# Full-array matmuls that may run as two half-width products side by side, so that the array keeps its column tiling

## The chip, the cores and the metric

The kernel runs on one NeuronCore of a Trainium2 chip. The metric is device time in microseconds for one launch, the median of several executions. The engines are named as in the profile: PE is the matrix engine (TensorE), PEld its weight loads, DVE the vector engine, ACT the scalar engine, POOL the GpSimd engine, SP the engine that issues most DMAs.

## What is computed

The input `x` has 2048 tokens of 576 features. It goes twice through a pair of blocks, with the same weights both times. Block A is attention over segments of 32 tokens with 8 memory tokens that are carried from segment to segment; block B is a gated MLP. Cut to what matters:

```
def A(x):                                  # x: 2048 x 576, already normalised
    mem = mem0                             # 8 x 576
    for s in range(64):                    # segments of 32 tokens
        h = concat(mem, x[32*s : 32*s+32])             # 40 x 576
        q, k, v = h @ Wq, h @ Wk, h @ Wv               # 32 heads of 128
        p = softmax(mask(q @ k.T * 128**-0.5))         # 40 x 40 per head
        o = (p @ v) @ Wo                               # 40 x 576
        mem, out[s] = o[:8], o[8:]
def B(x): return (silu(x @ w1) * (x @ w3)) @ w2        # 576 -> 4608 -> 576
x = x + A(layernorm(x)); x = x + B(layernorm(x))       # first layer
x = x + A(layernorm(x)); x = x + B(layernorm(x))       # second layer, same weights
```

A segment needs the memory rows of the segment before it, so the 64 steps of one layer are a chain.

## The kernel before

**Tiling and stages.** Time is cut into 72 steps `t`. In step `t` the kernel works on segment `t` of the first layer and on segment `t - 8` of the second (`LAG = 8`), as far as both exist; the two sit side by side, so that most products have 80 moving columns (2 x 40). In the first and the last steps only one layer is there and the products have 40. Per step there are four groups of eight heads, and for each group: Q and K projections (`QK`, 64 products with 128 contracted rows in two nodes, and `QKt`, the remaining 64 rows, as pairs in row tiling), scores (`SC`), softmax on DVE and ACT, a transposition of the probabilities as a matmul (`TR`), the product with V (`PV`), and the output projection (`WO`, 32 products, and `WOt`, the last 64 of the 576 output features, eight half-width products in column tiling). V itself is projected by `VX`, `VM` (column tiling) or `VG` (full array, with a row-tiled rest). Every four steps a piece of the MLP of both layers (`FF`, `FFt`, then `W2`, `W2b`) is spread between the attention work. Layer norms and the residual are transposed on PE too (`tr`, `POST`).

**Tiling of the array.** A matmul here uses the whole array (128 columns of weights), or a half of its columns (64 wide, at output partition 0 or 64: column tiling), or a half of its rows (64 contracted rows: row tiling), or quarters and smaller. Each PE node has a `mode` that says which: "full", "col", "row", "c32", "oct", "quad".

**What sets the order.** `make_nodes` makes a graph of nodes, each with an engine, a duration that is assumed, and what it needs and frees. `plan` walks through it. The order on PE is written out by hand: `ORDER` is a string with one letter for each PE node (`KINDS` gives the letters: Q, q, S, T, P, O, o, F, f, W, w, G, g, ...), made of `FIRST` (805 letters), eleven times `FOUR` (224 letters, four steps each) and `LAST` (684). For the other engines `plan` takes whichever node can start first by its assumed times; nodes of the kind "AD" (copies out of PSUM) go to ACT or DVE, whichever is free first. `plan` adds `SWITCH` (0.098 us) where the mode of a PE node differs from that of the one before. The emitter `Emitter` then writes the instructions in that order, each engine in program order; `mm` writes one matmul, and all PE instructions carry the line of that helper (L578; L581 is ACT's helper, L584 DVE's, L587 SP's, L593 POOL's).

**The end.** The last MLP piece has no attention beside it. Its weights don't go through the small double buffers, but are loaded into the space of Wq/Wk/Wv (`W`, `WV`) by `tail_load` in eight pieces of 512 columns, as soon as the last step has used that space. The finished rows are cast to bf16 by ACT (`fin_cast`) and stored.

Of the kernel before, what the change touches and what calls it, by code (L numbers as in the profile page):

```python
# [51 lines left out]
class Node:  # L52
# [3 lines left out]
    def __init__(self, eng, dur, fn, deps=(), prio=0.0, mode=None, acq=(), rel=(), name="", lat=None):  # L56
        self.eng, self.dur, self.fn, self.prio, self.mode = eng, dur, fn, prio, mode
        self.deps = [d for d in deps if d is not None]
        self.acq, self.rel, self.name = list(acq), list(rel), name
        self.lat = lat if lat is not None else (PE_LAT if eng == "PE" else EW_LAT)  # L60
        self.outs, self.ready, self.start, self.end, self.by = [], 0.0, None, None, None
        self.left = len(self.deps)
# [13 lines left out]
def plan(nodes, pools, letters):  # L76
# [16 lines left out]
    mode = None  # L93
    order = []
    at = 0
# [18 lines left out]
    while len(order) < len(nodes):  # L114
        best = None
        for e in t_eng:
            if e == "PE":
                cands = seq[at:at + 1] if at < len(seq) and seq[at].left == 0 else []
            else:
                cands = ready[e] + (both if e in ("ACT", "DVE") else [])  # L120
            if not cands:
                continue
            ests = [(est(e, n), n) for n in cands]
            t = min(x for x, _ in ests)
            if t >= NOW:
                continue
            if best is None or t < best[0]:
                best = (t, e, ests)
        if best is None:
            raise RuntimeError(f"the plan is stuck at {at}: {seq[at].name}")  # L130
        t, e, ests = best
        st, n = min((x for x in ests if x[0] <= t + 1e-9), key=lambda x: x[1].prio)
        dur = n.dur
        if isinstance(dur, tuple):
            dur = dur[0] if e == "ACT" else dur[1]
        if e == "PE":
            at += 1
            if n.mode != mode:
                dur += SWITCH
                mode = n.mode  # L140
        elif n.eng == "AD":
            both.remove(n)
        else:
            ready[e].remove(n)
        n.start, n.end, n.by = st, st + dur, e
        t_eng[e] = n.end
        for s in n.acq:
            if s.i is not None:
                continue
            f = free[s.pool]  # L150
            s.i = min((i for i in range(len(f)) if f[i] <= st + 1e-9), key=lambda i: f[i])
            f[s.i] = NOW
        for s in n.rel:
            s.users -= 1
            s.end = max(s.end, n.end + (PE_LAT if e == "PE" else EW_LAT))
            if s.users == 0:
                free[s.pool][s.i] = s.end
        for m in n.outs:
            m.ready = max(m.ready, n.end + (0.0 if m.eng == e == "PE" else n.lat))
            m.left -= 1  # L160
            if m.left == 0:
                push(m)
        order.append(n)
    return order
# [58 lines left out]
def make_nodes(em, nseg, pools, o=Opt, dma_bw=230e3, load_bw=400e3):  # L223
# [32 lines left out]
    m0t = node("PE", 0.3, em.m0_tr(b[0]), deps=[ld_m0], prio=-5, mode="full", acq=b, name="m0tr")  # L256
# [9 lines left out]
    def ln_nodes(tag, src, xn, deps, prio, writes, warm=False):  # L266

        a = node("DVE", 1.16, em.ln_stats(src, xn), deps=deps, prio=prio, acq=[] if src is xn else [xn], name=tag + "stats")
        p_ = node("POOL", 0.45, em.ln_pow(xn), deps=[a], prio=prio, name=tag + "pow")
        c = node("DVE", 0.46 if src is xn else 0.66, em.ln_norm(src, xn), deps=[p_], prio=prio, name=tag + "norm")  # L270
        b = Slot("bank", users=len(writes))
        d = node("PE", 5 * 0.056, em.ln_tr(xn, b, warm), deps=[c], prio=prio, mode="full", acq=[b], rel=[xn], name=tag + "tr")
        out = []
        for wr, cost, more in writes:
            out.append(node("AD", cost, wr(b), deps=[d] + more + out[-1:], prio=prio, rel=[b], name=tag + "wr"))
        return out
# [22 lines left out]
    def v_nodes(name, t, k, prio, tail_at, emit, strips, deps, tail_deps, free):  # L299
# [6 lines left out]
        for r in (0, 1):  # L306
            outs = em.v_parts(strips, r)
            b[r].users = len(outs)
            for p0, width, row, blk in outs:
                e = node("AD", ew(512), em.v_ev(b[r], p0, width, row, blk), deps=[m_, n] + free.get(blk // 2, []), prio=prio + 0.01 * (blk // 2),  # L310
                         rel=[b[r]], name=name + "e")
                vx_ev.setdefault((name, t, blk // 2), []).append(e)
# [6 lines left out]
    def vg_nodes(t, g, deps, tail_deps):  # L319
# [4 lines left out]
        m_ = node("PE", 8 * 0.2158, em.vg(t, g, b, False), deps=deps, prio=t + o.vm, mode="full", acq=b, name="VG")  # L324
# [5 lines left out]
    def vg_out(t, g, b, deps, row):  # L330

        return [node("AD", ew(512), em.v_ev(b[r], row, R64, row, 2 * g + r), deps=deps, prio=t + o.vm + 0.01 * g + (0.05 if row == 0 else 0.0), rel=[b[r]],
# [11 lines left out]
    def step(t):  # L344
# [17 lines left out]
        for g in range(NG):  # L362
            qs, qe = [], []
            for u in (2 * g, 2 * g + 1):
# [4 lines left out]
                          prio=pq, mode="full", acq=[q] + b, name="QK")  # L369
# [11 lines left out]
            sc = node("PE", 8 * 0.0165 * nl, em.scores(t, g, qs, s), deps=qe, prio=pf + o.sc, mode="col", acq=[s, sme], rel=qs, name="SC")  # L381
# [9 lines left out]
            tr = node("PE", 8 * mm80, em.ptr(t, g, pb, bt), deps=[pbs], prio=pf + o.tr, mode="full", acq=[pts] + bt, name="TR")  # L391
            node("POOL", 1.2, em.pb_zero(pb), deps=[tr], prio=pf, rel=[pb], name="pbz")
            pe_ = [node("AD", ew(4 * c80), em.pt_ev(t, g, m, bt[m], pts), deps=[tr], prio=pf, rel=[bt[m]], name="PTe") for m in (0, 1)]
            if paired(t):
# [6 lines left out]
                      prio=pf + o.pv, mode="full", acq=b + [ot], rel=[pts], name="PV")  # L401
# [4 lines left out]
            wo = node("PE", 32 * mm80, em.wo(t, g, ot), deps=ote + ([ld_o[g]] if t == 0 else []), prio=t + o.wo + o.wog * g, mode="full",  # L406
# [9 lines left out]
        if t == nst - 1:  # L416
            last_reads[2].extend(wos)
# [14 lines left out]
    def post(li, g):  # L432
# [4 lines left out]
                 prio=prio, mode="full", acq=b, name="POST")  # L437
# [3 lines left out]
    last_reads = [], [], []  # L441
    kept = {}

    def job(j):
# [18 lines left out]
        if last:  # L463
            v_done, qk_done, wo_done = last_reads
            tail = []
            for i in range(8):
                late = wo_done[i - 4:i - 3] if i >= 4 else []
                parts = [(0, 9 * 512, qk_done[2 * i:2 * i + 2] + late), (1, 4 * 576, v_done + late)]
                tail.append([load("tail", kb(128, c), s0 + o.tail_at + 0.01 * i, em.tail_load(i, what), deps=dep) for what, c, dep in parts])

        npp = NPR // 2
        for at, pp in enumerate([npp - 1] + list(range(npp - 1)) if last else range(npp)):
            mids, w2s, htts, lds = [], [], [], []
            stays = last and pp == npp - 1
            for pr_ in (2 * pp, 2 * pp + 1):
# [18 lines left out]
                fm = node("PE", 16 * mm, em.ffn_up(ents, pr_, w13, b, last and not stays, False), deps=wr + ld, prio=prio, mode="full",  # L494
# [8 lines left out]
            for (bi, g) in ents:  # L503
                b = banks()
                d = node("PE", 8 * 0.1225, em.ffn_down(bi, pp, htts, w2s, b, last and not stays), deps=mids + lds, prio=prio + o.w2,
                         mode="full", acq=b, rel=htts + w2s, name="W2b" if bi else "W2")
                es = [node("DVE", dve(288), em.ffn_add(g, h, xr[g], b[h]), deps=[d], prio=prio + o.w2, rel=[b[h]], name="W2a")
                      for h in (0, 1)]
                w2_last[bi] = es
        for (bi, g) in ents:  # L510
            if bi == 0:
                ht_set(1, g, ln_nodes("L1", xr[g], Slot("xn"), w2_last[0], s0 + LAG - 4.2, ht_writes(1, g)))
            else:
                xn = Slot("xn")
                c = node("ACT", actc(576), em.fin_cast(xr[g], xn), deps=w2_last[1], prio=s0 + LAG - 4.2, acq=[xn], rel=[xr[g]], name="fin")
                node("SWD", 1.0, em.store(g, xn, last), deps=[c], prio=s0 + LAG - 4.2, rel=[xn], lat=3.0, name="store")
# [42 lines left out]
class Emitter:  # L559


    def __init__(self, nc, tc, T, aps, nseg):
# [4 lines left out]
        self.tail_w, self.ys = {}, {}  # L567
# [9 lines left out]
    def mm(self, out, lhsT, rhs, start, stop, **k):  # L577
        self.ch("PE", self.nc.tensor.matmul(out, lhsT=lhsT, rhs=rhs, start=start, stop=stop, skip_group_check=True, **k))  # L578
# [107 lines left out]
    def tail_load(self, i, what):  # L686

        def f(n):
            T = self.T
            fa = i * 512  # L690
            t13, t2 = T.W[:, :, fa:fa + 512], T.WV[:, i * 4 * D:(i + 1) * 4 * D].rearrange("p (b d) -> p b d", b=4)
            if what != 1:
                for kind, wd in ((0, self.a.w1), (1, self.a.w3)):
                    self.dma(t13[:, 4 * kind:4 * kind + 4], wd[0:4 * P, fa:fa + 512].rearrange("(c p) f -> p c f", p=P))
                for kind, wd in ((0, self.a.w1), (1, self.a.w3)):
                    self.dma(t13[kind * R64:(kind + 1) * R64, 8], wd[4 * P:D, fa:fa + 512])
            if what != 0:
                self.dma(t2, self.a.w2[fa:fa + 512, :].rearrange("(b p) d -> p b d", p=P))
            for h in range(2):
                self.tail_w[2 * i + h] = (t13[:, :, h * 2 * P:(h + 1) * 2 * P], t2[:, 2 * h:2 * h + 2])  # L700
# [213 lines left out]
    def scores(self, t, g, qs, s):  # L914

        def f(n):
            S = self.bk(s)[:, 0:GH * QW].rearrange("p (h k) -> p h k", h=GH)
            both = self.both(t)
            for hl in range(4):
                for ab in (0, 1):  # L920
                    Q = self.T.QKT[:, qs[ab].i].rearrange("p a h n -> p (a h n)")
                    for kd in ((0, 1) if both else (0,)):
# [3 lines left out]
                                True, True, tile_position=(0, 64 * kd))  # L926
# [231 lines left out]
    def ffn_add(self, g, half, xr, b):  # L1158
        def f(n):
            X = self.T.XR[:, xr.i, half * 288:(half + 1) * 288]  # L1160
            self.v("scalar_tensor_tensor", X, self.bk(b)[:, 0:288], 0.5, X, op0=ALU.mult, op1=ALU.add)
        return f

    def fin_cast(self, xr, xn):
        return lambda n: self.act(self.T.XN[:, xn.i, 0:D], self.T.XR[:, xr.i, :], ACT.Copy)
# [10 lines left out]
def kernel(  # L1176
# [88 lines left out]
    for n in plan(nodes, pools, ORDER):  # L1265
        n.fn(n)
# [35 lines left out]
```

## Time and profile before

| | |
|---|---|
| median of 3 runs | 2701.22 us (2698.18 to 2702.51) |
| the profiled execution | 2705.47 us, of which its span is 2703.5 us |
| PE | 97% busy, 55,714 matmuls and 55,795 weight loads |
| DVE / ACT / POOL | 77% / 51% / 12% busy |
| granted PE clock | 0.992 |
| DMA | 321.40 MB, mean 119 GB/s |

The profile is one execution. A busy PE in it is a modelled figure: the end of a matmul is computed, so matmuls that follow each other closely overlap in the listing (one of 80 columns is listed with some 200 ns), and the distance from start to start tells the pace. The timeline view merges neighbours of the same kind, with the number of instructions after an x.

### The profile page before, as it was taken

How to read it: one execution, taken by the hardware profiler on the slowest of the kernel's cores; microseconds unless marked ns; L12 is line 12 of the kernel's file. 1: busy time of each engine (PE TensorE's matmuls, PEld its weight loads, DVE VectorE, ACT ScalarE, POOL GpSimd, SP SyncE). 2: the span in 40 equal slices, each digit the busy share in tenths (PEclk: the TensorE clock that was granted, in tenths of full speed). 3: DMA queues.
4: the chain of work that ended last, by engine and by line, in shares of the span. 5: the costliest groups of instructions: out<-in, count | busy, mean ns of one | idle time of the engine just before them, and what ended most of it. 6: DMA issues, size and time to landing. Idle time of an engine off the chain costs nothing.

```text
span 2703.5 us, 126553 instructions
## 1 busy us (share of the span) xinstructions
PE 2629.8 (97%) x55714; PEld 2227.4 (82%) x55795; DVE 2089.3 (77%) x5376; ACT 1370.6 (51%) x4025; POOL 333.5 (12%) x400
## 2 busy tenths in 40 slices
PE   5999999999999999999999999999999999999998
PEld 3788888888888888888888888888888888888886
DVE  4778887887778778777877877787787777787876
ACT  2655554544546454454645445464544546454553
POOL 1111110110101011010101101010110101011110
PEclk7999999999999999999999999999999999999999
DMA  9064534334343333434333343433334342434358
GB/s 316 4 176 120 158 89 119 88 110 125 93 131 88 115 92 110 125 95 130 87 114 93 110 125 93 131 88 112 94 110 125 93 131 71 125 97 135 117 164 258
DMA packets 483224, 321.40 MB, mean 119 GB/s; under 512 B 26376, under 2 KB 477328, under 8 KB 482160
## 3 DMA queue, kind: packets, MB, share of 16 engines
q1 hardware_dynamic: 479488, 306.22, 38.7%
q8 instruction: 436, 7.14, 1.1%
q0 software_dynamic: 3024, 6.93, 0.9%
q14 instruction: 116, 0.95, 0.1%
q10 hardware_dynamic: 160, 0.16, 0.0%
HBM read 308.49 MB, written 2.36 MB: 115 GB/s over the span
## 4 chain that ended last, share of the span: by engine, by line
PE 87%; ACT 4%; DMA 4%; DVE 3%; issue 1%; SPq 0%; POOL 0%; DVEq 0%; ACTq 0%; POOLq 0%
PE bank L578 87%; ACT V L581 3%; DMA W<-in_B_w_dram 2%; DVE SME L584 1%; DMA W<-in_A_Wk_dram 1%; DMA WV<-in_A_Wv_dram 1%; DVE STAT L584 1%; DVE V L584 1%; ACT SME L581 0%; SPq L587 0%; DMA W2C<-in_B_w_dram 0%; ACT XTB L581 0%; ACT PTS L581 0%; ACT QKT L581 0%; DVE PB L584 0%
## 5 line engine op out<-in xcount | busy, mean ns | idle before, releaser
L578 PEld LDWEIGHTS <-W 128*128 128x128 bf16 (+1 forms) x29520 | 1238.8, 98 | 150.6 <-issue 44.2
L578 PE MATMUL bank<-HT,W 128*128 128x80 bf16 (+3 forms) x23040 | 812.4, 197 | 23.7 <-DMA W<-in_A_Wq_dram 10.5
L578 PE MATMUL bank<-XTB,W 128*128 128x256 bf16 (+3 forms) x6480 | 661.3, 261 | 8.1 <-DMA W<-in_B_w_dram 6.9
L581 ACT ACTIVATE QKT<-bank 128x256 bf16<-128x256 f32 (+3 forms) x1587 | 367.6, 318 | 372.7 <-PE bank L578 353.8
L981 POOL MEMSET PB<- 128x1024 bf16 x288 | 274.1, 952 | 1820.1 <-PE bank L578 1317.4
L578 PE MATMUL bank<-OT,WO 128*128 128x80 bf16 (+3 forms) x11520 | 407.1, 198 | 1.1 <-issue 0.5
L581 ACT ACTIVATE V<-bank 64x512 bf16<-64x512 f32 (+1 forms) x616 | 347.3, 586 | 109.4 <-PE bank L578 104.2
L578 PEld LDWEIGHTS <-WO 128*128 128x128 bf16 (+1 forms) x11520 | 379.8, 102 | 16.1 <-issue 6.0
L578 PE MATMUL bank<-WV,HT 128*32 128x512 bf16 (+5 forms) x3160 | 356.9, 385 | 13.9 <-issue 8.5
L578 PE MATMUL bank<-W2C,HTT 128*128 128x288 bf16 x2240 | 315.4, 286 | 0.3 <-DMA W2C<-in_B_w_dram 0.2
L584 DVE TENSOR_TENSOR PB<-SME,STAT 40x128 bf16<-40x128 f32 (+4 forms) x912 | 274.8, 335 | 14.9
L584 DVE TENSOR_REDUCE STAT<-SME 104x8 f32<-104x320 f32 (+1 forms) x576 | 274.0, 476 | 13.9 <-ACT SME L581 8.5
L581 ACT ACTIVATE HTT<-bank 128x512 bf16<-128x512 f32 (+1 forms) x324 | 180.0, 557 | 180.7 <-PE bank L578 178.7
L578 PEld LDWEIGHTS <-HT 128*32 128x32 bf16 (+4 forms) x3240 | 137.1, 96 | 157.0 <-issue 38.5
L584 DVE SCALAR_TENSOR_TENSOR XR<-bank,XR 128x288 f32<-128x288 f32 x576 | 246.5, 450 | 15.8 <-PE bank L578 7.9
L578 PEld LDWEIGHTS <-HTT 128*128 128x128 bf16 x2304 | 209.8, 98 | 49.1 <-issue 0.9
L581 ACT ACTIVATE OT<-bank 128x320 bf16<-128x320 f32 (+1 forms) x398 | 149.7, 406 | 167.9 <-PE bank L578 166.5
L584 DVE CAST QKT<-bank 128x192 bf16<-128x192 f32 (+2 forms) x461 | 124.9, 317 | 137.7 <-PE bank L578 136.2
L584 DVE SCALAR_TENSOR_TENSOR HTT<-HTT,bank 128x512 bf16<-128x512 bf16 (+1 forms) x324 | 202.5, 625 | 33.7 <-ACT HTT L581 29.6
L584 DVE TENSOR_TENSOR HTT<-HTT,bank 128x512 bf16<-128x512 bf16 (+1 forms) x324 | 203.6, 628 | 30.6 <-DVE HTT L584 0.5
L581 ACT ACTIVATE PTS<-bank 128x320 bf16<-128x320 f32 (+1 forms) x385 | 144.9, 403 | 161.6 <-PE bank L578 123.9
L581 ACT ACTIVATE SME<-SME 104x320 f32<-104x320 f32 (+1 forms) x288 | 135.9, 472 | 138.1 <-DVE SME L584 135.6
(61 smaller groups left out, 1804.4 us busy)
## 6 DMA issues: line engine op xcount, KB each, us to landing
W<-in_B_w_dram SPq DMA_DIRECT2D x612, 256.0 KB, 3.6
W2C<-in_B_w_dram SPq DMA_DIRECT2D x306, 288.0 KB, 3.3
W<-in_B_w_dram SPq DMA_DIRECT2D x612, 32.0 KB, 3.3
W<-in_B_w_dram SPq DMA_DIRECT2D x16, 512.0 KB, 8.8
WO<-in_A_Wo_dram SPq DMA_DIRECT2D x4, 1152.0 KB, 16.1
XR<-in_A_x_dram POOLq DMA_DIRECT2D x16, 288.0 KB, 2.9
WV<-in_B_w_dram SPq DMA_DIRECT2D x8, 576.0 KB, 7.3
W<-in_A_Wq_dram SPq DMA_DIRECT2D x8, 512.0 KB, 8.7
```

Of the source, the lines that this page charges most:

```text
L578: self.ch("PE", self.nc.tensor.matmul(out, lhsT=lhsT, rhs=rhs, start=start, stop=stop, skip_group_check=True, **k))
L581: self.ch("ACT", self.nc.scalar.activation(*a, **k))
L584: self.ch("DVE", getattr(self.nc.vector, fn_)(*a, **k))
L981: return lambda n: self.ch("POOL", self.nc.gpsimd.memset(self.T.PB[:, pb.i], 0.0))
```

## The change

The PE order string stays as it is. The change has five parts.

1. A mode may name alternatives: "full/col". Nodes that were "full" and have more than half of the array's columns (`QK`, `TR`, `PV`, `WO`, `FF`, `W2`, `VG`, the transpositions) become "full/col", and so do the scores of steps with one layer, which use 40 columns. `plan` walks along PE and keeps the set of modes that are still possible; where a node has none of them, it adds `SWITCH`, and gives all nodes since the last switch the first mode that is left to them (`settle`). A stretch of "full/col" nodes that holds a "col" node, such as scores of two layers or a `WOt`, thereby runs in column tiling as a whole.
2. `Emitter.mm` writes a product of a node that got "col", and that has no tile position of its own, as two products: output partitions 0 to 63 and 64 to 127, each with 64 columns of the weights and the same moving operand.
3. Assumed durations: copies of V out of PSUM get 0.55 (ACT) or 0.6 (DVE) instead of those that `ew(512)` gives; scores of steps with one layer get 8 x 0.029.
4. The cast `fin_cast` on ACT goes away. The last two additions of the second layer's MLP write bf16 rows into the store's buffer `XN` themselves.
5. The weights of the last MLP piece come in four pieces of 1024 columns instead of eight of 512, and none of them waits for `WO` any more.

```diff
@@ Node
-        self.eng, self.dur, self.fn, self.prio, self.mode = eng, dur, fn, prio, mode
+        self.eng, self.dur, self.fn, self.prio, self.mode = eng, dur, fn, prio, mode.split("/") if mode else mode
@@ plan
-    mode = None
+    mode, run = [], []
     order = []
+
+    def settle():
+        for x in run:
+            x.mode = mode[0]
+        run.clear()
...
-            if n.mode != mode:
+            if not any(m in mode for m in n.mode):
                 dur += SWITCH
+                settle()
                 mode = n.mode
+            mode = [m for m in mode if m in n.mode]
+            run.append(n)
...
         order.append(n)
+    settle()
     return order
@@ make_nodes
-                e = node("AD", ew(512), em.v_ev(b[r], p0, width, row, blk), deps=[m_, n] + free.get(blk // 2, []), prio=prio + 0.01 * (blk // 2),
+                e = node("AD", (0.55, 0.6), em.v_ev(b[r], p0, width, row, blk), deps=[m_, n] + free.get(blk // 2, []), prio=prio + 0.01 * (blk // 2),
...
-                          prio=pq, mode="full", acq=[q] + b, name="QK")
+                          prio=pq, mode="full/col", acq=[q] + b, name="QK")
...
-            sc = node("PE", 8 * 0.0165 * nl, em.scores(t, g, qs, s), deps=qe, prio=pf + o.sc, mode="col", acq=[s, sme], rel=qs, name="SC")
+            sc = node("PE", 8 * (0.0165 * nl if nl == 2 else 0.029), em.scores(t, g, qs, s), deps=qe, prio=pf + o.sc, mode="col" if nl == 2 else "full/col", acq=[s, sme], rel=qs, name="SC")
...
@@ make_nodes, job
-            for i in range(8):
-                late = wo_done[i - 4:i - 3] if i >= 4 else []
-                parts = [(0, 9 * 512, qk_done[2 * i:2 * i + 2] + late), (1, 4 * 576, v_done + late)]
-                tail.append([load("tail", kb(128, c), s0 + o.tail_at + 0.01 * i, em.tail_load(i, what), deps=dep) for what, c, dep in parts])
+            for i in range(4):
+                parts = [(0, 9 * 1024, qk_done[4 * i:4 * i + 4]), (1, 8 * 576, v_done)]
+                tail += [[load("tail", kb(128, c), s0 + o.tail_at + 0.01 * i, em.tail_load(i, what), deps=dep) for what, c, dep in parts]] * 2
...
-                es = [node("DVE", dve(288), em.ffn_add(g, h, xr[g], b[h]), deps=[d], prio=prio + o.w2, rel=[b[h]], name="W2a")
-                      for h in (0, 1)]
+                fin = Slot("xn") if bi and at == npp - 1 else None
+                es = [node("DVE", dve(288), em.ffn_add(g, h, xr[g], b[h], fin), deps=[d], prio=prio + o.w2, acq=[fin] if fin and h == 0 else [],
+                           rel=[b[h]] + ([xr[g]] if fin and h else []), name="W2a") for h in (0, 1)]
...
-                xn = Slot("xn")
-                c = node("ACT", actc(576), em.fin_cast(xr[g], xn), deps=w2_last[1], prio=s0 + LAG - 4.2, acq=[xn], rel=[xr[g]], name="fin")
-                node("SWD", 1.0, em.store(g, xn, last), deps=[c], prio=s0 + LAG - 4.2, rel=[xn], lat=3.0, name="store")
+                xn = fins.pop(g)
+                node("SWD", 1.0, em.store(g, xn, last), deps=w2_last[1], prio=s0 + LAG - 4.2, rel=[xn], lat=3.0, name="store")
@@ Emitter
     def mm(self, out, lhsT, rhs, start, stop, **k):
+        if self.mode == "col" and "tile_position" not in k:
+            for r in (0, R64):
+                self.mm(out[r:r + R64], lhsT[:, r:r + R64], rhs, start, stop, tile_position=(0, r), **k)
+            return
...
@@ scores
-                                True, True, tile_position=(0, 64 * kd))
+                                True, True, **({"tile_position": (0, 64 * kd)} if n.mode == "col" else {}))
@@ ffn_add
-            self.v("scalar_tensor_tensor", X, self.bk(b)[:, 0:288], 0.5, X, op0=ALU.mult, op1=ALU.add)
+            self.v("scalar_tensor_tensor", self.T.XN[:, fin.i, h] if fin else X, self.bk(b)[:, 0:288], 0.5, X, op0=ALU.mult, op1=ALU.add)
```

The other lines of the diff put "full/col" for "full" in the same way, double the sizes in `tail_load`, and set `em.mode` from each node before it is written.

## The prediction

> **What bounds the kernel now.** I read the page's shares first, then the waits, then short stretches of the timeline on PE, because the change touches PE's order of tilings and little else.
>
> ```profile
> PE 2629.8 (97%) x55714; PEld 2227.4 (82%) x55795; DVE 2089.3 (77%) x5376; ACT 1370.6 (51%) x4025; POOL 333.5 (12%) x400
> ```
>
> PE is the bound: 97% busy, DVE 77%. The waits say how much of its time is waiting: of PE's own rows the largest are 12.8 us for "issue" in 57 pieces and 10.5 us for the first load of Wq. So time comes out of the kernel only if PE's own work gets shorter, and what PE saves the others must follow. By stage:
>
> ```profile
> 0.00:130.00 130.00, 95.07 (x2672) 76.41 (x2673) 76.51 (x211) 55.48 (x161) 22.30 (x36) 0.86 0.50 166
> 1161.00:1318.50 157.50, 156.13 (x3121) 132.60 (x3127) 123.59 (x314) 80.82 (x238) 18.56 (x23) 1.00 0.37 108
> ```
>
> (Columns: window, length, busy us of PE, PEld, DVE, ACT and POOL, PE clock, DMA share, GB/s.) The second line is one repeat of the order's middle part; the long pieces of the chain of waits recur every 157.5 us (73.51 us of PE from 597.14, from 754.72, from 912.22). PE waits 1.4 us of it by the listing. The first 130 us are different: PE idles 35 of them. What the busy time consists of, from start to start:
>
> ```profile
> 1201.42 0.38 PE L578 MATMUL bank<-XTB,W 64*128 64x256 bf16 x4
> 1201.73 1.32 PE L578 MATMUL bank<-HT,W 128*128 128x80 bf16 x32
> 1202.98 0.43 PE L578 MATMUL bank<-QKT 128*64 128x40 bf16 x16
> ...
> 1234.12 1.32 PE L578 MATMUL bank<-OT,WO 128*128 128x80 bf16 x32
> 1235.27 0.45 PE L578 MATMUL bank<-PTS,V 128*128 128x80 bf16 x8
> ...
> 1237.95 0.77 PE L578 MATMUL bank<-OT,WO 128*64 128x80 bf16 x32
> 1238.65 0.42 PE L578 MATMUL bank<-W2C,HTT 128*128 128x288 bf16 x2
> ```
>
> 32 Wo products of 80 columns that stay in full tiling take 1235.27 - 1234.12 = 1.15 us, 35.9 ns each. 32 Q/K products that are followed by column-tiled scores take 1202.98 - 1201.73 = 1.25 us: **the change of tiling costs 0.10 us**. The same from row to full: the row pairs ahead take 1201.73 - 1201.42 = 0.31 us, and two pairs of 256 columns account for 0.22 (the full products of 256 columns follow each other at 109 ns). Single starts, read in the same way over all adjacent nodes, give 93 to 101 ns for full to column, full to row, row to column and column to row. The last two lines give the price of half-width work: 16 pairs (32 products) took 0.70 us including the switch out (0.10) and a slower start (first pair 53 ns, second 41), so 35.9 ns a pair in between: **a pair of half products with 80 columns costs what a full product costs.** With 40 columns it doesn't:
>
> ```profile
> 2654.09 0.96 PE L578 MATMUL bank<-OT,WO 128*128 128x40 bf16 x32
> 2654.89 0.36 PE L578 MATMUL bank<-PTS,V 128*128 128x40 bf16 x8
> ...
> 183.82 0.56 PE L578 MATMUL bank<-OT,WO 128*64 128x40 bf16 x24
> 184.31 0.42 PE L578 MATMUL bank<-W2C,HTT 128*128 128x288 bf16 x2
> ```
>
> A full product takes 0.80/32 = 25 ns; 12 pairs took 0.49 us with the switch and the slow start (0.12), so some 31 ns (the starts in the middle of the run are 31.7 apart).
>
> [...]
>
> **Part 1, switches.** I applied the rule of the diff to the order's string, letter by letter (each letter's old and new modes; a switch where no mode is left). Switches fall from 1296 to 856: opening 321 to 210, each of the eleven repeats 65 to 42, closing part 259 to 183. Most of those that stay lead into and out of the row-tiled rests. At 98 ns: 11 x 23 x 0.098 = 24.8 us, 111 x 0.098 = 10.9, 76 x 0.098 = 7.4; **43.1 us less**. The slow start after a switch into column tiling (22 ns) is paid 232 instead of 326 times: 2.1 us less. All this lies on PE, the bound.
>
> **Part 2, what is split.** By the same count 30,913 products become pairs: 21,408 of 80 columns, 3,184 of 256, 2,024 of 288, 592 of 512, 657 of 128, and 3,048 of 40. For 80 the row is the pair above, difference 0. For 128 to 512 the nearest row is the column-tiled V product of 512 columns (a pair every 217 ns beside 216 in full): I take 0; at most 1 ns each, 6 us; below nothing is excluded, since a pair streams the same columns. For 40 columns 6.7 ns each: 3048 x 6.7 = 20.4 us, of which 1,848 products (12.4 us) are in the opening and 1,200 (8.0 us) in the closing part. Of the opening's 90 such nodes 51 lie before 150 us, where PE idles a quarter of the time; I take 9 of the 12.4. Sum **17 us more**, at least 8 and at most 20. Scores of one layer keep their pace (25 ns a product now and in full); their gain is among the switches.
>
> **Parts 3 to 5.** The assumed copy times of V (ACT measured 587 ns, DVE 685) move some of 864 copies between ACT and DVE and can't be priced: 0, from -5 to +10 us, covered by ACT's 49% idle time; without that cover DVE, at 77%, would be late with 0.69 us a copy. The casts are 16 of 685 ns on ACT, off the path save the last one: between the last DVE addition (ends 2699.68) and the store (2700.42) stands only this cast, so 0.7 us less. The earlier store rows hold one of two `XN` buffers longer, which POOL's store queue sees and PE doesn't. The tail's DMAs run at 332 to 357 GB/s from 2660 to 2690, the rate and not the wait for `WO` sets them; PE waits for them 1.21 and 2.32 us near the end. Fewer, larger issues on SP leave the bytes the same; the last piece then feeds four instead of two column blocks after its landing, and can start a little earlier: 0, from -4 to +4 us.
>
> **What is given back.** A repeat becomes 2.3 us shorter. At its step boundaries PE already waits some 0.3 to 0.5 us for the copies of the memory rows, and those waits don't shrink with PE's work. DVE would go from 123.6 of 157.5 to 123.6 of 155.2 (80%). I take 3 us over the kernel.
>
> **Sum.** -43.1 - 2.1 + 17 - 0.7 + 3 = -26 us. Against the profiled execution, 2705.47 us (span 2703.5 and 2.0 around it), that is 2679.5; it stood 4.25 us above the median, and the median of 2701.2 becomes **2675 us**, 1.0% less.
>
> **Rivals.**
> 1. *PE runs out of instructions* (slower). A full product is a weight load and a matmul; a pair is four instructions in 35.9 ns, 9.0 ns each. The program grows from 111,500 to some 173,400 PE instructions. The trace shows 9 ns only in runs of 64 instructions (the 32 half products above, with their loads)[...]; in longer runs the densest is the full product of 40 columns, 12.5 ns an instruction. In its favour: nothing shows 9 ns sustained over the several hundred instructions of the new runs. Against it: the pairs don't slow down toward the end of a run, and the fetched blocks (7.14 MB in 1.1% of 16 engines' time, 476 us) come at 15 GB/s where 7.1 would be needed. Price: at 10 ns an instruction each of 21,408 pairs costs 4 ns more, 86 us: 2675 + 86 = 2761 us. It decides from 26 / (21,408 x 4), 0.3 ns above 9.0.
> 2. *The saving turns into waits* (same). Each step ends in a chain (last `WOt`, copies of the memory rows, next `QK`), and copies feed every node. If these don't move up with PE, only the parts between boundaries gain: with nine tenths of 26 us lost, 2699 us. Against it: PE waits 1.4 us in 157.5, so it is not the chain that paces.
> 3. *The new plan is worse on ACT and DVE* (slower). New assumed times and switches reassign the copies, while the PE order was laid out for other times. 3 us more waiting per repeat is 33: 2708 us. Against it: idle time on both engines.
> 4. *The change doesn't do what it says.* If a switch were only moved, or column to row cost 128 ns instead of 98 (the pairs after scores can be read so), 220 such switches would add 7 us: 2682. This is in the main case's range.
>
> **How the numbers follow.** Main case 0.68, range 2652 (the costs of 40 columns hidden, no giving back, tail and copies at their good ends) to 2692 (the bad ends). Rival 2 has 0.09, rival 1 0.15, rival 3 0.08. About 5 us, 0.2%, is what a measurement of this kernel can tell from no change. Faster: the main case, and 0.02 of rival 2, 0.70. Same: the rest of rival 2, 0.07. Slower: rivals 1 and 3, 0.23. The range goes up to 2715 to take in rivals 2 and 3; it leaves out most of rival 1.
>
> **What would show it.** Right: 86,600 matmuls; a repeat of 155 us; `WO`, `QK` and `PV` as 128*64 with 80 columns in pairs of 36 ns through a whole run; PE still at 97%. Wrong: pairs that fall to 40 ns and more after the first sixteen (rival 1), "issue" waits of PE beyond 13 us; repeats of 157 us with longer waits for ACT or DVE (2 and 3).

## The result, and the profile after

The changed kernel takes **3084.62 us** (median of 4 runs, 3079.81 to 3087.4) beside 2701.38 for the kernel before (4 runs): a ratio of 1.1417, with a 95% interval from 1.14 to 1.1434. 2675 us was predicted, 1.0% less than before. The profiled execution took 3084.38 us, 3082.6 of it span. The page's shares of engines and its queue of instructions:

```profile
PE 2734.4 (89%) x86684; PEld 2384.2 (77%) x86708; DVE 2133.1 (69%) x5523; ACT 1329.6 (43%) x3862; POOL 333.3 (11%) x400
...
q8 instruction: 678, 11.11, 1.5%
```

There are 86,684 matmuls, close to the 86,600 that were forecast, but PE is no longer busy all the time: 89% where it was 97%. The page of before has 436 instruction packets; here there are 678:

```profile
q8 instruction: 436, 7.14, 1.1%
```

One repeat of the order's middle part now takes 177.7 us where it took 157.6 (the distance of the same instruction of POOL, four steps on, over eleven repeats). The view of windows (columns as in the prediction) for one repeat:

```profile
577.00:755.00 178.00, 159.37 (x5105) 139.31 (x5102) 122.76 (x315) 77.25 (x225) 18.54 (x22) 0.98 0.33 94
```

PE stands still for 18.6 us of the 178, where it was 1.4 of 157.5. The difference of the spans falls into 88 us up to step 12, 222 in the next eleven repeats and 70 after them: it is everywhere, and not at one place. What PE waits for, from the list of waits (total us, times, longest), first in the changed kernel, then in the one before:

```profile
PEld L591 <- issue: 420.3, 694, 3.0
...
PE bank L591 <- issue: 242.1, 249, 2.9
...
PE bank L591 <- DVE XN L597: 31.6, 14, 4.9
```

```profile
PE bank L578 <- issue: 12.8, 57, 1.6
```

"issue" was 12.8 us in 57 pieces on PE; now it is 242.1 in 249. (PEld's line overlaps PE's; the two aren't added. More than half of the 12.8 isn't real: the trace of before lacks 81 of 55,795 matmul records, and 49 of the 57 pieces are gaps of 0.16 us where such a record is missing. The kernels with parts 3 to 5 alone and with the times of V's copies alone, below, have all records, and 8.0 us in 10 pieces and 5.7 in 8.) "issue" says that nothing in the profile held PE back: no semaphore, no buffer. The timeline of PE shows how these waits lie:

```profile
2096.55 0.98 PE L591 MATMUL bank<-OT,WO 128*64 128x80 bf16 x45 [0.78 <-issue]
2097.36 0.46 PE L591 MATMUL bank<-PTS,V 128*64 128x80 bf16 x16
2097.65 1.15 PE L591 MATMUL bank<-W2C,HTT 128*64 128x288 bf16 x16
2098.63 1.09 PE L591 MATMUL bank<-OT,WO 128*64 128x80 bf16 x51
2100.57 0.98 PE L591 MATMUL bank<-OT,WO 128*64 128x80 bf16 x45 [0.84 <-issue]
...
2109.70 0.63 PE L591 MATMUL bank<-HT,W 128*64 128x80 bf16 x25 [2.26 <-issue]
2110.16 0.38 PE L591 MATMUL bank<-QKT 128*64 128x40 bf16 x15
2110.37 0.20 PE L591 MATMUL bank<-HT,W 128*64 128x80 bf16 x1
2110.38 0.19 PE L591 MATMUL bank<-QKT 128*64 128x40 bf16 x1
2110.40 1.75 PE L591 MATMUL bank<-HT,W 128*64 128x80 bf16 x86
2113.45 2.59 PE L591 MATMUL bank<-HT,W 128*64 128x80 bf16 x128 [1.29 <-issue]
2117.19 0.19 PE L591 MATMUL bank<-HT,W 64*128 64x80 bf16 x1 [1.15 <-issue]
```

Count the matmuls between one stop and the next: 45 + 16 + 16 + 51 = 128, 25 + 15 + 1 + 1 + 86 = 128, and 128 again. With their weight loads these are 256 instructions, whatever they compute and wherever a node ends: **one stop per block of 256 instructions**. (The page agrees: 86,684 matmuls and 86,708 weight loads came with 678 instruction packets, 255.7 to a packet.) Within a block the pairs keep their pace: 64 pairs in the line of 128, listed with 2.59 us, of which the last product's own 0.2 is the end; some 37 ns a pair. (The granted clock is 0.971 in the mean, 0.992 before; since the pace within the blocks is nearly the 36 ns of before, the clock isn't what makes the time.) When new instructions arrive is seen in the DMA view of 2094 to 2120 us (40 slices of 0.65 us; the third line is the instruction queue's count, MB and share):

```profile
DMA  4000000000010058999984111100000100000000
GB/s 142 0 0 0 0 0 25 0 0 0 0 25 0 0 60 291 287 353 262 324 268 130 35 32 52 25 0 0 0 0 0 25 0 0 0 0 0 0 25 0
...
q8 instruction: 7, 0.11, 1.9%
```

Each lone "25" (25 GB/s x 0.65 us = 16 KB) is one block of instructions on its way. In the trace the fetches start at 2094.23, 2098.14, 2101.73, 2106.92, 2110.87 and 2114.64 us, and PE resumes 2.3 to 2.9 us after each. Over the whole kernel two fetches never start closer than 3.23 us (median 4.15); in the kernel before never closer than 3.27 (median 5.91). A packet itself takes 1.04 us in the median. So between two fetches the instruction queue shows no packet for some 2.2 us and more (3.23 less 1.04).

The whole trace shows the same cycle. Of the "issue" waits of PE 228 are longer than 0.3 us. Each of them ends 2.1 to 3.1 us after the start of a fetch, and the next fetch starts 1.04 us after that end at the soonest, 1.16 us in the median. The two least parts (2.15 and 1.04) add up to 3.2 us, close to the least spacing. Why the next fetch isn't started while PE still waits for the one before, no run here shows.

### The profile page after: what moved, and what is told of

Same layout as the page of the kernel before. It is cut to its first block, busy times and chain, and to the rows that moved or that the text cites. A ratio compares the mean times of both kernels' runs of the same rounds, so it can differ in the third digit from the quotient of the medians.

```text
span 3082.6 us, 188313 instructions
## 1 busy us (share of the span) xinstructions
PE 2734.4 (89%) x86684; PEld 2384.2 (77%) x86708; DVE 2133.1 (69%) x5523; ACT 1329.6 (43%) x3862; POOL 333.3 (11%) x400
## 4 chain that ended last, share of the span: by engine, by line
PE 77%; issue 9%; DVE 6%; DMA 4%; ACT 3%; SPq 1%; DVEq 0%; POOL 0%; ACTq 0%
PE bank L591 77%; ACT V L594 2%; DMA W<-in_B_w_dram 2%; DVE SME L597 1%; SPq L600 1%; DVE STAT L597 1%; DVE PB L597 1%; DMA W<-in_A_Wk_dram 1%; DVE V L597 1%; DMA WV<-in_A_Wv_dram 1%; DVE XN L597 0%; DVE HTT L597 0%; ACT SME L594 0%; DVE LNS L597 0%; DMA W2C<-in_B_w_dram 0%
## 5 line engine op out<-in xcount | busy, mean ns | idle before, releaser
L591 PEld LDWEIGHTS <-W 128*64 128x64 bf16 (+2 forms) x45632 | 1335.0, 110 | 270.5 <-issue 195.7
L591 PE MATMUL bank<-HT,W 128*64 128x80 bf16 (+5 forms) x35616 | 874.8, 201 | 134.2 <-issue 112.7
L591 PE MATMUL bank<-XTB,W 128*64 128x256 bf16 (+5 forms) x10016 | 679.0, 265 | 32.2 <-issue 18.1
L594 ACT ACTIVATE QKT<-bank 128x64 bf16<-128x64 f32 (+2 forms) x1510 | 349.8, 314 | 539.4 <-PE bank L591 519.8
L591 PE MATMUL bank<-OT,WO 128*64 128x80 bf16 (+3 forms) x19680 | 431.1, 200 | 55.2 <-issue 53.1
L591 PEld LDWEIGHTS <-WO 128*64 128x64 bf16 (+1 forms) x19680 | 403.8, 113 | 69.7 <-issue 65.7
L594 ACT ACTIVATE V<-bank 32x512 bf16<-32x512 f32 (+1 forms) x594 | 336.9, 585 | 127.2 <-PE bank L591 120.4
L591 PE MATMUL bank<-WV,HT 128*32 128x512 bf16 (+4 forms) x3809 | 374.3, 392 | 9.5 <-issue 4.4
L591 PE MATMUL bank<-W2C,HTT 128*64 128x288 bf16 (+1 forms) x4264 | 330.0, 290 | 17.6 <-issue 16.6
L591 PEld LDWEIGHTS <-HTT 128*64 128x64 bf16 (+1 forms) x4328 | 250.9, 111 | 41.4 <-issue 24.1
## 6 DMA issues: line engine op xcount, KB each, us to landing
W<-in_B_w_dram SPq DMA_DIRECT2D x8, 1024.0 KB, 12.8
```

The source lines that it names most:

```text
L594: self.ch("ACT", self.nc.scalar.activation(*a, **k))
```

## The experiments

The theory (A in the expectations): PE can't be given more than one block of 256 instructions in some 3.3 to 4 us (the author's estimate from the starts of the fetches, 3.23 us apart at the least and 4.15 in the median), and column pairs at 9 ns an instruction use up a block in 2.3. Rival theories: pairs in column tiling are slow in themselves in long runs (B); the new plan for ACT and DVE, or parts 3 to 5, make the loss (C).

**The rate by itself.** A kernel that leaves the whole computation out and runs long stretches of products of one kind on PE, on fixed operands (one run):

```
full("full80", 80, 1024);  col("col80", 80, 768);  row("row80", "rowb80", 80, 768)
col("col128", 128, 768);   full("full40", 40, 1536)
...                        # then 40 loads of 256 KB beside:
col("stream80", 80, 1024)
```

> This kernel leaves the whole computation out (its output is a copy of x); it runs stretches of matmuls on fixed operands with no waits between them, each in its own PSUM tile: full80 (1024 full products of 80 columns), col80 (768 pairs of column-tiled halves of 80 columns, 3072 instructions with the weight loads), row80 (768 pairs of row-tiled halves of 80 columns, 3072 instructions), col128 (768 column pairs of 128 columns), full40 (1536 full products of 40 columns), stream80 (1024 column pairs of 80 columns with 40 DMAs of 256 KB beside them). Theory A, PE starves for instructions because a block of 256 of them can't be fetched in less than some 3.3 us (the least distance between two fetches in both traces): full80 36.7 us at 36 ns a product; col80 12 x 3.3 = 40 us instead of 27.6, in bursts of 36 ns a pair with pauses once per 256 instructions; row80 the same 40 us, though it isn't column-tiled; col128 43 us, its own pace of 56 ns a pair, no pauses; full40 39 to 40 us; stream80 53 to 64 us. Rival B, column tiling itself is slower when it is sustained [...]: col80 about 38 us but evenly, without pauses, col128 about 13 ns a pair slower than 56, so 53 us, and row80 at 27.6 us. Rival C, the new plan on ACT and DVE is at fault and not PE's instructions: all stretches at their own pace, col80 and row80 27.6 us.

Groups of PE by line and form (busy us, mean ns, then idle before and its releaser):

```profile
L55 PE MATMUL col<-XT,WT 128*64 128x128 bf16 x1536 | 44.0, 219 | 1.1 <-issue 1.1
L55 PE MATMUL stream<-XT,WT 128*64 128x80 bf16 x2048 | 42.4, 208 | 23.1 <-issue 23.1
L49 PE MATMUL full<-XT,WT 128*128 128x40 bf16 x1536 | 40.4, 179 | 2.2 <-issue 1.8
L49 PE MATMUL full<-XT,WT 128*128 128x80 bf16 x1024 | 36.9, 202 | 0.0
L55 PE MATMUL col<-XT,WT 128*64 128x80 bf16 x1536 | 29.8, 202 | 13.6 <-issue 13.6
...
L62 PE MATMUL rowb<-XT,WT 64*128 64x80 bf16 x768 | 29.7, 198 | 13.6 <-issue 13.6
```

The 768 row pairs, the tiling the kernel uses for its rests, idle the same 13.6 us as the 768 column pairs, so column tiling isn't slow in itself. 768 pairs are 3,072 instructions, 12 blocks; up to the start of what comes next the column pairs took 43.4 us, 3.62 us a block, 14.1 ns an instruction, where their own pace would give 27.6 us. That includes a start without stops: PE stops for the first time after 183 column products. From then on a block takes 3.78 us in the mean; of the row pairs it takes 3.58, a small difference that stays unexplained. 1,024 full products of the same size took 36.7 us, 36 ns each and so 4.6 us a block, without a stop. Pairs of 128 columns (56 ns by their own pace, 3.6 us a block) wait 1.1 us in 12 blocks. And full products of 40 columns, 1,536 in 42.6 us, are limited too: 27.7 ns each where their own pace is 25. With transfers beside (the "stream" line) the stops grow from 13.6 us in 12 blocks to 23.1 in 16. The loads run beside the first 39 of its 65 us only: in that time, and while the granted clock was full, fetches start 4.1 to 5.4 us apart; after the loads 3.4 to 3.8. Timeline of the quiet stretch, then of the one with loads:

```profile
63.85 2.48 PE L55 MATMUL col<-XT,WT 128*64 128x80 bf16 x128 [1.24 <-issue]
67.58 2.48 PE L55 MATMUL col<-XT,WT 128*64 128x80 bf16 x128 [1.24 <-issue]
```

```profile
245.74 2.49 PE L55 MATMUL stream<-XT,WT 128*64 128x80 bf16 x128 [2.89 <-issue]
250.29 3.56 PE L55 MATMUL stream<-XT,WT 128*64 128x80 bf16 x128 [2.07 <-issue]
```

128 matmuls, a stop, 128 matmuls: this is the pattern of the changed kernel, with no other compute engine at work. (In the last line the pairs themselves are slower, 3.56 us: the granted clock was 0.5 from 251.4 to 254.8 us.)

**The whole change without splitting.** Products stay whole; the new plan and parts 3 to 5 stay.

```diff
     for n in plan(nodes, pools, ORDER):
-        em.mode = n.mode
         n.fn(n)
```

> The changed kernel with the split of products not written out: the mode chosen by the plan isn't handed to the writer of matmuls, so every product is full again, and the plan of all engines, the shorter list of casts and the four tail pieces stay as changed. Theory A (instruction supply): the time comes back to that of the kernel before, 2690 to 2702 us. Rival B (column tiling slow in itself): the same. Rival C (new plan on ACT and DVE, parts 3 to 5): stays far above, 2800 us or more.

Measured 2758.68 us, 1.0204 (1.0187 to 1.0221): between the two expectations, and outside both. Without the split 326 us of the loss are gone, but 57 remain that neither theory had. PE's waits and its timeline:

```profile
PE bank L591 <- DVE XN L597: 33.5, 13, 5.3
PE bank L591 <- issue: 14.3, 58, 2.2
```

```profile
682.41 0.45 PE L591 MATMUL bank<-ident,XN 128*128 128x128 bf16 x5 [2.40 <-DVE XN L597]
```

"issue" is back at 14.3 us. What is new is a wait of 2.40 us for a layer norm, about once in each repeat. The norm of the same place, first in the kernel before and then here (POOL's power of the variance, DVE's normalisation):

```profile
662.44 0.55 POOL L741 TENSOR_TENSOR LNS<-LNS,mhalf 128x1 f32<-128x1 f32 x1 [11.93 <-DVE LNS L584]
...
664.58 0.57 DVE L584 TENSOR_SCALAR XN<-XR,LNS 128x576 bf16<-128x576 f32 x1
```

```profile
676.67 0.55 POOL L754 TENSOR_TENSOR LNS<-LNS,mhalf 128x1 f32<-128x1 f32 x1 [11.93 <-DVE LNS L597]
...
680.30 1.05 DVE L597 TENSOR_TENSOR PB<-SME,STAT 40x320 bf16<-40x320 f32 x3
681.38 0.49 DVE L597 TENSOR_TENSOR SME<-bank,maskb 104x320 f32<-104x320 f32 x1
681.78 0.57 DVE L597 TENSOR_SCALAR XN<-XR,LNS 128x576 bf16<-128x576 f32 x1
```

Before, DVE normalises 1.6 us after POOL is done (662.99 to 664.58); now 4.6 us after (677.22 to 681.78), because the plan put softmax work of two groups and copies ahead of it. That the plan's order is the reason is read from DVE's queue; that norm wasn't moved by itself. But `plan` keeps its own clock, and run on the two kernels without a chip it says the same: by its assumed times the whole kernel takes 2652 us in the order of before and 2688 in the changed one, and a repeat 156.5 and 158.4, since PE now waits 3.07 us in it for this norm, though it has 23 switches less. The late norm was thus planned, and could be read before any run.

**The split without parts 3 to 5.** The kernel before with parts 1 and 2 only.

```diff
-            if n.mode != mode:
+            if not any(m in mode for m in n.mode):
...
+        em.mode = n.mode
```

> The kernel before with parts 1 and 2 alone (alternative modes, split products); the V copy times, the casts and the eight tail pieces stay as before. Theories A and B: 3070 to 3095 us. Rival C, as far as parts 3 to 5 make the loss: near 2700 us.

Measured 3080.37 us (one run), as expected: parts 1 and 2 alone make the whole loss.

**Fewer splits.** In the changed kernel the Q/K products may not be split (13,208 products are split, where it was 30,913).

```diff
-                          prio=pq, mode="full/col", acq=[q] + b, name="QK")
+                          prio=pq, mode="full", acq=[q] + b, name="QK")
```

> The changed kernel with the Q/K projections left full: 13,208 products are split instead of 30,913, and 1100 switches of tiling are left instead of 856. Theory A, priced as blocks of 256 instructions that take at least 3.9 us each (the value that gives the changed kernel its time): 2701 + 142 = 2843 us, between 2800 and 2860. Rival B, evenly 13 ns for each split pair: 2701 + 175 - 10 = 2866 us. Rival C: still about 3085 us.

Measured 2821.86 us (one run), in the range of the theory, 44 us below what rival B gives. PE waits:

```profile
PE bank L591 <- issue: 75.8, 102, 3.2
...
PE bank L591 <- DVE XN L597: 7.9, 3, 5.3
```

This is as the theory of the fetch has it: whole products among the pairs stretch a block's time, and the stops fall from 242.1 to 75.8 us. (The plan differs too: the late norms are nearly gone, 7.9 us.)

**The split on the old plan.** `plan` and the order of every engine as before; only then are modes given by the new rule and products split.

```diff
+    placed = plan(nodes, pools, ORDER)
...                                    # can = ["full", "col"] where mode was "full"
+        if not any(m in mode for m in can):
+            settle()
+            mode = can
...
+    for n in placed:
+        em.mode = n.mode
```

> The kernel before, with ACT, DVE, POOL and DMA in the order of its own plan, and only the writing of PE changed: the tilings follow the rule of the change, so the same 30,913 products are split. Theory A (instruction blocks pace PE; the new plan's late layer norms are a second, separate cost of about 30 to 57 us): 3030 to 3055 us, no waits of PE for XN beyond the 6 us of before. Theory A alone, without a cost of the plan: 3080 us.

Measured 3035.65 us (2 runs), 1.1228 (1.1207 to 1.1248), 332 us above before, and within the expectation. The waits, with the norm's line of before beside them:

```profile
PE bank L584 <- issue: 255.1, 269, 2.8
...
PE bank L584 <- DVE XN L590: 5.9, 2, 5.1
```

```profile
PE bank L578 <- DVE XN L584: 6.2, 3, 5.2
```

The stops are all there and the late layer norms are gone (5.9 us, before 6.2). So **the split costs 332 us, and what the rest of the change adds to it is 49**; alone that rest is 57.

**Parts 3 to 5 alone**: the changed kernel with modes as before.

```diff
-                          prio=pq, mode="full/col", acq=[q] + b, name="QK")
+                          prio=pq, mode="full", acq=[q] + b, name="QK")
...                                    # and so for all others; SC again "col"
```

> The changed kernel without parts 1 and 2: all modes as before, no splits; the V copy times, the shorter casts and the four tail pieces are kept. If the 57 us of the run with the plan alone come from the planned switches: 2690 to 2703 us. If they come from the V times, the casts or the tail: 2740 to 2760 us.

Measured 2719.43 us, 1.0053 (1.0039 to 1.0067): 16 us slower than before, between the two expectations and outside both. The repeats take 157.58 us as before; the loss is 8.6 us up to step 12 and 6.7 after the repeats.

**A chosen split.** On the old plan, only stretches are split where a sum with 3.9 us a block says that it pays: 2,674 products instead of 30,913; 1187 switches (before 1296, changed 856).

```diff
+    for n, c in zip([n for n in placed if n.eng == "PE"], SPLIT):
+        if c == "c":
+            n.mode = "col"
...
+    for n in placed:
+        em.mode = n.mode
```

> The kernel before with its own plan, and column tiling kept only in stretches that were chosen so that the blocks of 256 instructions there don't fall below 3.9 us: 2,674 products split, 1186 switches instead of 1296, scores of one layer in full. Theory A: 9 us less than before, 2692 us (2688 to 2697). Rival B (evenly 13 ns for each split pair): 2701 - 11 + 35 = 2725 us.

Measured 2699.96 us (21 runs beside 33 of before, 2703.42): 0.999 (0.9983 to 0.9996). The 2688 to 2697 that were expected are missed. It is the only version that is measurably below the kernel before, and by 3 us where 109 switches of 0.098 us promise 11. A repeat has three switches less and takes 157.48 us instead of 157.58 (one trace of each): of 0.3 us it keeps 0.1. The stops don't take the rest: "issue" is 4.3 us in 6 pieces. PE's waits for ACT's copies of V grow from 3.0 to 5.1 us; the remainder isn't traced.

**The same with parts 4 and 5.**

```diff
-                c = node("ACT", actc(576), em.fin_cast(xr[g], xn), deps=w2_last[1], prio=s0 + LAG - 4.2, acq=[xn], rel=[xr[g]], name="fin")
+                xn = fins.pop(g)
...
-            for i in range(8):
+            for i in range(4):
```

> The kernel with the same chosen stretches and with the shorter casts and the four tail pieces of the change, V copy times as before: 1 to 3 us less than with the chosen stretches alone, 2690 us.

Measured 2702.15 us, 0.9995 (0.9987 to 1.0004): no gain, where 1 to 3 us were expected. Parts 4 and 5 don't cost the 16 us of parts 3 to 5 either, which leaves the assumed times of V's copies.

**These times alone**, and then **the plan's new rule alone** (with the assumed time of one-layer scores, which the repeats don't have), nothing split, in the kernel before:

```diff
-                e = node("AD", ew(512), em.v_ev(b[r], p0, width, row, blk), deps=[m_, n] + free.get(blk // 2, []), prio=prio + 0.01 * (blk // 2),
+                e = node("AD", (0.55, 0.6), em.v_ev(b[r], p0, width, row, blk), deps=[m_, n] + free.get(blk // 2, []), prio=prio + 0.01 * (blk // 2),
```

> The kernel before with one thing of part 3 alone: the assumed times of the copies of V are 0.55 (ACT) and 0.6 us (DVE). Theory: these times are what cost e5 its 16 us, since they move copies from ACT to DVE: 2719 us (2715 to 2723), repeats of 157.6 us as before, and the loss in the opening and at the end. Rival: the loss of e5 comes from the store rows or the tail's pieces after all: 2700 to 2706 us here.

Measured 2713.44 us, 1.0046 (1.0029 to 1.0063), a little below the 2715 to 2723 of the theory and well above the rival's 2706: about 10 of the 16 us come from there, though only 19 more copies go to DVE (267 where it was 248). PE then waits 7.7 us in 9 pieces for DVE's `PB`, before 0.9 us in 3.

```diff
-            if n.mode != mode:
+            if not any(m in mode for m in n.mode):
...                                    # modes "full/col"; em.mode isn't set
```

> The kernel before with the new rule for switches in the plan alone (and the assumed time of one-layer scores), nothing split, the old V times, store and tail. Theory: the plan's loss in e1 (57 us) is the sum of two parts, 16 us of V times and 41 us of layer norms that the plan puts late on DVE because it no longer expects some switches: 2743 us (2736 to 2750), repeats of 160.2 us with one wait of about 2.4 us for XN each. Rival: the late layer norms come from the V times and the rule together: 2700 to 2712 us here, repeats of 157.6 us.

Measured 2781.79 us, 1.0294 (1.0279 to 1.0309): 79 us more than before, not 41, and outside both expectations. A repeat takes 163.1 us, and PE waits in it for more than the norm:

```profile
1208.40 0.19 PE L591 MATMUL bank<-HT,W 64*128 64x80 bf16 x1 [0.82 <-ACT V L594]
1209.41 0.30 PE L591 MATMUL bank<-HT,W 64*128 64x80 bf16 x7 [0.82 <-ACT QKT L594]
...
1333.45 0.47 PE L591 MATMUL bank<-ident,XN 128*128 128x128 bf16 x5 [2.40 <-DVE XN L597]
```

2.40 + 0.82 + 0.82 = 4.04 of the 5.5 us. So the parts don't add up: parts 3 to 5 cost 16 us on the old plan and take 23 back on the new one (2781.8 with the rule alone, 2758.7 with them). What is settled is that the new rule's plan is late, and that the rule alone does it: by `plan`'s own clock the repeat of this kernel takes 159.4 us, again with 3.07 us for the norm. How parts 3 to 5 take 23 us back isn't settled.

## Why the prediction was wrong, by its steps

**The step that failed is the 0 for 80 columns in Part 2**, and with it the dismissal of rival 1. The pace of 35.9 ns a pair was right within a block: the quiet kernel shows 36 ns, the changed one some 37. What it was read from, 64 instructions, is a quarter of a block. It doesn't hold over blocks: a block of 256 instructions at 9 ns lasts 2.3 us, and the next one comes after 3.6 to 3.8 us in the quiet kernel of products alone, up to 5.4 with loads beside. If each block of the order takes the greater of its own time and 3.6 us, the sum of the split is some +275 us; with 3.9 us it is some +380. The 332 measured lie at some 3.8 us a block, the 3.78 of the quiet column pairs (an estimate from Part 2's paces and the blocks of the traces). The same estimate gives the kernel before 5 to 13 us.

**The argument against rival 1 was wrong in kind.** It divided 7.14 MB by the time of the packets and had 15 GB/s. A packet does take 1.04 us, but the next isn't started for another 2 us or more: 16.4 KB in 3.62 us is 4.5 GB/s, below the 7.1 needed. A sign of it stood in the trace of before: 436 fetches, no two starts closer than 3.27 us, which is 12.8 ns an instruction, above the 9.0 of the pairs. Even "the full product of 40 columns, 12.5 ns an instruction" was a pace of short runs: over 1,536 of them it is 27.7 ns a product, 13.9 an instruction. That "the pairs don't slow down toward the end of a run" was true of 16 pairs and says nothing of the stop between blocks. **Rival 1's price** of 10 ns was picked close to the 9.0; the stretches show 14.1 ns sustained, which is 56 ns a pair where 40 was assumed. Of its two signs, pairs of 40 ns and more didn't come, since the pairs keep their pace and then stop; the "issue" waits beyond 13 us did.

**Part 1** counted right (its parts add to 1295 and 855, since the first node isn't in them), but a removed switch isn't worth its 98 ns: in the chosen split each repeat keeps 0.1 of 0.3 us, the whole kernel 3 of 11. "What is given back" was thus too small as well: 3 of 45 us were assumed, and some two thirds were given back in the chosen split. That fits rival 2; where most of it goes isn't shown. **Parts 3 to 5** were put at 0, from -5 to +10; together they cost 16 us, outside it, and about 10 of it are the V times. The cast is gone as said: the last addition ends at 3079.76 us and the store starts at 3079.78, 0.02 us where 0.74 stood; in the medians this can't be seen. **Rival 3** was right in its mechanism and mis-sized: 2.6 us a repeat and 57 in all without the split, where 3 us and 33 had been put down, at a chance of 0.08. The argument against it, idle time on both engines, says nothing on the order: DVE was 77% busy in the kernel before, and the new order still gave a norm 3 us later. The prediction ran the rule of the switches over the order's string, but not `plan` itself, whose clock shows the longer repeat.

## What to carry to other kernels

Count instructions, not only columns: before a product is cut into pairs, work out from the paces of the new form how long 256 PE instructions (matmuls and weight loads) last, and compare it with the closest spacing of instruction fetches in the trace (3.2 to 3.4 us here, 3.6 to 3.8 when it lasts). In the quiet kernel pairs of 80 columns, 2.3 us a block, stood still for 13.6 us in 12 blocks, and full products of 80 columns, 4.6 us a block, didn't. A pace that was read from fewer instructions than a block was no evidence for longer runs: 9.0 ns an instruction over 64 became 14.1 over 3,072. And when the times that a planner assumes change, the other engines' order changes too: read the planner's own clock for both orders first, then test the new order with the old instructions, and the new instructions in the old order.

## What the runs showed of the hardware that was not expected

- PE's instructions come in blocks of 256, one fetch after the other, with starts 3.23 us apart at the least in the changed kernel (173,392 matmuls and weight loads in 678 packets). In a quiet kernel 12 blocks took 43.4 us, 14.1 ns an instruction. While loads of 256 KB ran, and the clock was full, starts were 4.1 to 5.4 us apart.
- A stop ends 2.1 to 3.1 us after the start of a fetch, and the next fetch starts 1.04 us after that end at the soonest (228 stops of the changed kernel).
- The sign is sharp: "issue" waits of PE, up to 2.9 us long, with 128 matmuls and so 256 instructions from stop to stop, or a multiple of it (within three matmuls for all but one of the distances between 228 stops; 24 matmul records are missing).
- Column pairs and row pairs are nearly alike in this: 43.3 and 43.2 us from the first start to the last of 768 pairs of 80 columns.
- A full product of 40 columns takes 25 ns in a short run and 27.7 over 1,536.
